# Row maxima of a block-sparse attention kernel taken from products of high parts, in two 64-row tiles of TensorE, from the twelfth unit on

## The chip, the cores and the metric

The program runs on one core of a Trainium2 chip. The time is the device time of one execution in microseconds (us); several executions are taken and their median is compared. A core has TensorE (PE in the profile; its weight loads are listed apart as PEld), VectorE (DVE), ScalarE (ACT), GpSimd (POOL) and SyncE (SP, which issues nearly all DMAs here). TensorE multiplies a stationary operand of up to 128 rows and 128 columns, the weights, with a moving operand that streams past it; results go to PSUM.

## The reference

Attention with a block mask, over 4 batches, 8 heads, 768 positions and a head size of 64, and then a two-layer network over the joined heads:

```
scores = scale * q @ k.T                       # 768 x 768 for each batch and head
mask   = neighbours, first and last block of 32, and 3 sampled blocks for each block of queries
scores = where(mask, scores, -1e9)
scores = scores - max(scores, axis=-1)
attn   = exp(scores) / (sum(exp(scores)) + 1e-9)
x      = attn @ v                              # heads joined: 3072 x 512
h      = x @ w_in                              # 3072 x 2048
out    = (h * clip(h + 3, 0, 6) / 6) @ w_out   # 3072 x 512
```

The row maximum cancels out of `attn` up to rounding: any number near it serves to keep `exp` in range.

## The kernel before, in words

**Number formats.** Most products are made in two or three parts. A value x is split into a high part (x rounded to fp32r, a format that TensorE takes in one pass) and a low part (x minus its high part, again fp32r). The products of attention weights with v (`av`) and the sums of exponentials (`dm`) take plain fp32 operands.

**Units.** The attention is done in 64 units, u0 to u63, one for each batch, half of the queries (384 of them) and head. A unit's steps are methods of the class `Unit`:

- `loadq`, `loadk`, `loadv`: DMAs on SP's queue. q arrives transposed and stacked twice, so that partitions 0 to 63 and 64 to 127 hold the same 64 x 384 numbers (`qraw`, one buffer, so that the next `loadq` waits for the last reader of this one). k likewise (`kraw`).
- `qh` (ACT) writes q/8 rounded, its high part, into all 128 partitions of `QA`; `ql` (DVE) then overwrites partitions 0 to 63 with the low part. `kh` (ACT) writes k's high part into both halves of `KA`. So one product of QA with KA over 128 rows gives (low q + high q) x high k.
- `m_0`, `m_1`, `m_2` (line 573): for a third of the unit's queries each, two matmuls with QA as weights and KA moving, 384 columns of keys each, into the two PSUM banks of one tile named `big`. Query 3p+t stands in row p of third t, so the weights are read with a step of three elements. Units 1 to 8 use other PSUM tiles (`early`).
- `r_0` to `r_2` (DVE) reduce each `big` tile to the maxima of the 24 blocks of keys; `fin` adds the mask and reduces to one maximum for each query, `mt` brings the maxima as a row into `qb` (by a DMA from the tenth unit on).
- `s_0` to `s_2`: the scores themselves, transposed, four matmuls each: KA x QA, and `kb` x `qb`, which holds low k x high q, the mask and the maxima in 97 rows. `e` (ACT) takes exp of each `big` tile of scores into `pr` (a pool of 14 buffers).
- `av` (line 636): 12 products of two units at once, one unit's result in PSUM partitions 0 to 63, the other's in 64 to 127, that is, in two column tiles of TensorE of 64 columns; `dm` (line 648): sums over keys for four rows at once, in four column tiles of 32. Both are fp32, so each product is two instructions.

**The network** runs as 64 steps, m0 to m63: `h_00` to `h_11` (x times w_in, 384 columns, three matmuls for each of four pieces), `ga`, `gb`, `gh`, `gl` (activation and split), `o_00` to `o_21` (times w_out, 512 columns, three matmuls each). The weights are split into parts in the first quarter of the run (steps w0 to w31).

**What sets the order.** The string `SCORE` lists every step of every unit in the order that a planner gave them; `play` (line 823) walks it and each engine issues in exactly that order. A step that has not been issued when something needs it is issued then. The pool `big` has two tiles, so `m`, `s`, `h` and `dm` share two PSUM tiles of two banks.

Of the kernel before, what the change touches and what calls it, by code (L numbers as in the profile page):

```python
# [35 lines left out]
BYDMA = 10  # L36
QUICK = "0 1 2 3 4 5 6 7 8 9 10 11 12 13 14 15 16 17 18 19 20 21 22 23 24 25 26 27 28 29 30 31"
# [8 lines left out]
    loadk kh kl qb; u1 fin_0; w2 bits_2; u2 ql m_0; w1 low; w0 high; w3 load; u0 e_2; u1 fin_1 mt qm; u2 r_0; w3
    size; u2 m_1; k0 kb_1; u1 s_0; u2 r_1; u1 s_1; w3 bits_0 bits_1 bits_2; u2 m_2 r_2; u1 e_0 e_1; w5 load size
    bits_0; u1 s_2 e_2 dm; u2 fin_0; w5 bits_1; u3 loadq qh ql qb loadk kh; u2 loadv fin_1 mt qm; w5 bits_2; w4 load;
    u0 loadv; u1 dc; u3 m_0 r_0; u2 s_0; w0 low; u3 m_1 r_1; u2 e_0; u4 loadq; w6 load; w4 size bits_0 bits_1; u2 s_1
    s_2 e_1 e_2; u3 m_2 r_2 fin_0; w4 bits_2; w3 high; w6 size; w3 low; u3 fin_1 kl; u4 loadk; w6 bits_0; w2 high; u1  # L50
    av; u4 qh ql; u1 rg rc; u3 mt; u4 qb; w6 bits_1; w1 save; u4 kh kl; u3 qm; u4 m_0; u3 s_0 e_0; u1 uc; w7 load; u4
    r_0 m_1 r_1; u3 s_1 s_2; w6 bits_2; u4 m_2; w7 size; u3 e_1 e_2; u4 r_2 fin_0; w7 bits_0; u3 av; u4 loadv; u5
    loadq qb qh; u4 fin_1 mt; u5 loadk kh; w7 bits_1 bits_2; w6 high; u5 ql m_0; w2 low; w8 load; u5 r_0; w3 save; u3
    uc; w8 size; w10 load; w8 bits_0 bits_1; w6 low; w8 bits_2; u4 qm; w7 high; u3 dm dc; u5 m_1 r_1; u4 s_0 s_1; w5
    high; u4 e_0; u1 rs; u5 m_2 r_2 kl; w10 size; u4 e_1; u6 loadq; u5 fin_0 fin_1; u4 s_2; u6 qh loadk ql kh; u5 mt
    qm; u6 m_0 r_0; u5 s_0; w7 low; u4 e_2; u6 m_1 r_1 kl qb; u5 e_0; w8 high; u5 s_1; w9 load; u3 rg; w5 low; u5
    s_2; w10 bits_0; u5 loadv; w6 save; u6 m_2; u5 e_1 e_2 dm; w9 size; u1 rb; u6 r_2 fin_0 fin_1 mt; w10 bits_1
    bits_2; u3 rc; u5 dc; u7 loadq qh; u5 av; u7 ql loadk kh m_0; w12 load; w9 bits_0 bits_1; u7 qb; u3 rs; w9
    bits_2; u6 qm; w4 high; u6 s_0 e_0; u7 kl; u8 loadq; u7 r_0; w4 low; u6 s_1; u7 m_1 r_1; u6 s_2; u7 m_2 r_2
    fin_0; u6 e_1; u8 qb; u6 e_2; u8 loadk; u5 rg; u7 loadv fin_1 mt; u8 qh; u6 loadv; u8 ql; u5 rc; u8 kh m_0 r_0;  # L60
    u7 qm; w8 low; w12 size; u5 uc; u7 s_0 e_0; w9 high; u8 m_1 r_1; w11 load size; u5 rs; u7 s_1; u1 ux_0; u7 s_2
    e_1 e_2; u9 loadq; w4 save; w11 bits_0; w12 bits_0; u8 m_2 r_2; w11 bits_1; w12 bits_1; u8 kl; u9 qh qb; u3 rb;
    u1 ux_1; u7 av; w11 bits_2; w12 bits_2; w5 save; u5 rb; u8 fin_0 fin_1 mt; w9 low; u9 ql; u7 dm; u5 ux_0; u1
    ux_2; w12 high low; u9 loadk; w14 load; u8 qm; u9 loadv kh; u7 dc; u9 kl m_0 r_0; w16 load; u9 m_1 r_1; w14 size
    bits_0; u8 s_0 s_1; w7 save; w2 save; w10 high; m0 loadin_0; w10 low; w14 bits_1; w11 high; w9 save; u10 loadq;
    w8 save; u8 e_0 s_2; u7 rg; u8 e_1 e_2; u10 qb; u9 m_2; u3 ux_0; w14 bits_2 high; u5 ux_1; w11 low; u7 rc; u9 r_2
    fin_0; w14 low; u9 fin_1; u10 loadk; u9 mt; u10 qh kh ql; u9 qm; m1 loadin_1; w16 size; m1 loadin_0; u5 ux_2; u10
    kl m_0 m_1 r_0 r_1; w12 save; u7 rs; w16 bits_0; u3 ux_1; u7 uc; u9 s_0 e_0 s_1 e_1; w16 bits_1; w18 load size;
    u3 ux_2; m0 h_00 loadin_1; w14 save; u11 loadq; w16 bits_2; w18 bits_0 bits_1; w11 save; u7 rb; w16 high; u9 s_2;
    m0 loadout_1; w10 save; u7 ux_0; m0 h_10; u9 e_2; u7 ux_1; m0 loadout_0; u10 m_2; w18 bits_2; u7 ux_2; u8 loadv;  # L70
    u10 r_2; u11 qh; w18 high low; u11 ql; m0 h_01; u10 fin_0; u11 qb; m0 h_11 ga; u11 loadk; w13 load; u11 loadv;
    w13 size; w15 load size; u11 kh; m1 h_00 h_10; w16 low; m1 loadout_1; u10 fin_1 mt loadv; w16 save; m0 gb gh; m1
    h_01 h_11; w13 bits_0 bits_1 bits_2; w15 bits_0; m0 gl; m3 loadin_1; w15 bits_1 bits_2; w13 high low; u10 qm s_0
    e_0; w17 load; w18 save; u9 av; m1 ga gb; w15 high low; w19 load; w17 size bits_0 bits_1; u9 dm dc; u12 loadq;
    u10 s_1; w19 size bits_0; m0 o_00; u10 e_1 s_2 e_2; w17 bits_2 high; m2 loadin_1; u11 m_0; m0 o_10 o_20; u11 kl;
    m1 gh gl; u12 loadv; m2 loadin_0; w13 save; w19 bits_1; u12 loadk; w20 load; w15 save; m2 loadout_0; u12 qh kh;
    u11 r_0; w19 bits_2; u12 qb; u11 m_1 r_1; m1 loadout_0; u11 m_2; m0 o_01 o_11; u9 rg; w22 load; w17 low; m2 h_00
    h_01; u12 kl ql; u11 r_2; w19 high; u13 loadk loadq; w20 size bits_0; u11 fin_0; w20 bits_1 bits_2; u11 fin_1;
    w17 save; m2 h_10 h_11; u12 m_0; u11 mt; m0 o_21; m1 o_00; w21 load; u13 loadv; m2 loadout_1; u12 r_0; m2 ga gb;
    w20 high; w22 size; m2 gh; m1 o_10; w22 bits_0; u12 m_1 r_1 m_2 r_2 fin_0; m4 loadin_1; u12 fin_1 mt qm; m1 o_20;  # L80
    w20 low; w22 bits_1; m1 o_01; m3 loadin_0; u11 qm s_0 s_1; w19 low; m1 o_11; u11 e_0 e_1; w21 size; w22 bits_2;
    w21 bits_0; m3 loadout_0; u11 s_2; m2 gl; u13 qh; u11 e_2; u13 ql; m1 o_21; w22 high; w21 bits_1 bits_2; u13 qb;
    w20 save; w24 load; m2 o_00; u13 kh kl; u14 loadq; w22 low; m2 o_10; u12 s_0 s_1; w22 save; u12 e_0 e_1; m2 o_01;
    u13 m_0 r_0; u12 s_2 suma; m2 o_11; u9 uc; u12 e_2; w24 size; u13 m_1; m3 h_00 h_10; u13 r_1; u14 qh; w24 bits_0
    bits_1 bits_2; u13 m_2; u14 ql; m3 h_01; u14 loadk kh kl; w26 load; u13 r_2; w19 save; w23 load; u13 fin_0; m3
    h_11; w21 high; u13 fin_1; m4 loadin_0; u13 mt; m3 ga gb; w0 save; w26 size bits_0; m5 loadin_0; u13 qm; w21 low
    save; w26 bits_1 bits_2; u14 m_0; u11 av; u14 r_0; u11 dm; u14 qb loadv; m5 loadin_1; w28 load; w23 size; w24
    high; w23 bits_0 bits_1; u12 sumb; u11 dc; m2 o_20; w26 high; u14 m_1 r_1; u12 sumc; m3 gh; w26 low; w24 low; u13
    s_0; w23 bits_2; u13 e_0; u15 loadq; m2 o_21; u13 s_1 e_1; m4 h_00 h_10; u15 loadk; u14 m_2; m4 h_01 h_11; w26
    save; u14 r_2; w30 load; u14 fin_0 fin_1 mt; u13 suma; u9 rc; w28 size bits_0; m3 loadout_1 gl; u11 uc; m4 ga gb;  # L90
    u13 s_2; u15 qb; u9 rs; m4 loadout_1; w23 high low save; u13 e_2 av; m4 gh; w28 bits_1; u15 qh; w28 bits_2; u15
    ql kh kl m_0; w30 size; u14 qm; u15 m_1 r_0 r_1; m3 o_00; u15 loadv; m3 o_10; u14 s_0 e_0; w30 bits_0; w27 load;
    u14 s_1 e_1; w27 size; m3 o_20; u13 sumb; m4 loadout_0; u13 uc; u16 loadq; m3 o_01; u11 rg; w24 save; u13 sumc;
    u15 m_2; u16 loadk; m5 h_00 h_10; u15 r_2; m4 gl; w30 bits_1; u9 rb; w30 bits_2; u14 s_2; w28 high; w27 bits_0;
    u15 fin_0 fin_1; u16 qb; m5 h_01; w31 load; u15 mt; u11 rc; u16 qh ql; w27 bits_1; u14 e_2; w28 low; u16 kh kl;
# [775 lines left out]
```

## Time and profile before

| | us |
|---|---|
| median of 3 runs | 958.35 |
| lowest and highest | 954.04, 960.99 |
| the profiled execution | 959.63, of which 957.8 from the first to the last instruction |
| PE busy | 927.6 |
| DVE busy | 601.9 |
| ACT busy | 442.4 |
| POOL busy | 243.3 |

Busy time of PE counts overlapping matmuls once. A matmul's recorded duration includes its way through the array, so a row of "338 ns" for 384 columns does not say how often one can start; the starts in the timeline do.

### The profile page before, as it was taken

The page shows a single profiled execution, that of the slowest core. Times are in us where ns is not written, and L with a number is a line of the kernel's source. Part 1 is how long each engine was busy: PE and PEld are TensorE (multiplying, and loading weights), DVE is VectorE, ACT ScalarE, POOL GpSimd, SP SyncE. Part 2 cuts the span into 40 slices and gives each one's busy share as a digit, 9 for nine tenths or more (in the row PEclk, how much of TensorE's full clock was granted, in tenths as well). Part 3 has the DMA queues.
Part 4 walks back from the last instruction along what each step waited for, and adds up shares of the span by engine and source line. Part 5 has one row for each costly group of instructions (what it writes and reads, how often), then busy time and mean ns, then how long its engine had stood idle before and what let it go on. Part 6 is the DMA issues. An engine that isn't in the chain of part 4 may idle for free.

```text
span 957.8 us, 13375 instructions
## 1 busy us (share of the span) xinstructions
PE 927.6 (97%) x4894; PEld 766.2 (80%) x4894; DVE 601.9 (63%) x875; ACT 442.4 (46%) x674; POOL 243.3 (25%) x145
## 2 busy tenths in 40 slices
...
GB/s 228 203 179 245 230 308 228 231 221 192 126 126 173 143 145 129 177 104 178 149 143 125 172 175 103 147 140 163 184 103 155 164 150 140 125 147 72 187 110 88
DMA packets 97125, 155.84 MB, mean 163 GB/s; under 512 B 24618, under 2 KB 45226, under 8 KB 97060
## 3 DMA queue, kind: packets, MB, share of 16 engines
...
q8 instruction: 38, 0.62, 0.3%
...
## 4 chain that ended last, share of the span: by engine, by line
PE 86%; DVE 6%; DMA 4%; issue 1%; ACT 1%; POOL 0%; SPq 0%; ACTq 0%; DVEq 0%
PE big L321 48%; PE out L321 28%; PE av L321 10%; DVE bm L321 2%; DVE xhl L321 2%; DVE QA L321 1%; DMA kraw<-kT 1%; DMA wout_lo<-xhl 1%; DMA wraw<-w_out 1%; DVE acc L321 0%; DMA qb<-mneg 0%; DMA vo<-vP 0%; ACT KA L321 0%; DMA spread<-rec 0%; DVE spread L321 0%
## 5 line engine op out<-in xcount | busy, mean ns | idle before, releaser
L321 PE MATMUL big<-xhl,win_hi 128*128 128x384 f32 x1024 | 263.2, 338 | 0.0
L321 DVE TENSOR_REDUCE bm<-big 128x24 f32<-128x768 f32 x168 | 159.6, 954 | 139.1 <-PE big L321 137.3
L321 POOL TENSOR_TENSOR glo<-g,ghi 128x768 fp32r<-128x768 f32 x64 | 120.4, 1882 | 398.3 <-ACT ghi L321 382.1
L321 ACT ACTIVATE pr<-big 128x768 f32<-128x768 f32 x192 | 151.7, 811 | 129.1 <-PE big L321 128.5
L321 POOL TENSOR_TENSOR kb<-kraw,KA 64x768 fp32r<-64x768 f32 x64 | 121.4, 1897 | 306.5 <-ACT KA L321 263.3
L321 PEld LDWEIGHTS big<-xhl,win_hi 128*128 128x128 f32 x1024 | 187.5, 188 | 4.9 <-issue 1.2
L321 PE MATMUL big<-xhl,wlo_in 128*128 128x384 f32 x512 | 173.6, 339 | 0.0
L321 PE MATMUL out<-wout_hi,ghi 128*128 128x512 f32 x384 | 151.7, 395 | 0.0
L321 PE MATMUL out<-wout_hi,glo 128*128 128x512 f32 x384 | 151.4, 394 | 0.0
L321 PE MATMUL out<-wlo_out,ghi 128*128 128x512 f32 x384 | 151.2, 394 | 0.0
L321 PE MATMUL big<-QA,KA 128*128 128x384 f32 x384 | 136.3, 355 | 0.7 <-DVE bm L321 0.5
L321 PE MATMUL big<-qb,kb 97*128 97x384 f32 x384 | 134.8, 351 | 0.7 <-DMA qb<-mneg 0.4
L321 ACT ACTIVATE g<-big,half_b 128x768 f32<-128x768 f32 x64 | 57.7, 902 | 161.3 <-PE big L321 140.5
L321 PE MATMUL av<-pr,vo 128*64 128x384 f32 x768 | 131.4, 492 | 0.0
L321 DVE SCALAR_TENSOR_TENSOR g<-g,big 128x768 f32<-128x768 f32 x64 | 60.7, 949 | 97.7 <-ACT g L321 97.7
L321 PEld LDWEIGHTS av<-pr,vo 128*64 128x64 f32 x768 | 52.5, 137 | 65.8 <-issue 64.3
L321 PE MATMUL big<-KA,QA 128*128 128x384 f32 x336 | 91.0, 358 | 10.1 <-ACT KA L321 5.3
L321 PEld LDWEIGHTS big<-KA,QA 128*128 128x128 f32 x336 | 75.8, 255 | 27.3 <-issue 8.0
L321 PEld LDWEIGHTS big<-xhl,wlo_in 128*128 128x128 f32 x512 | 96.4, 188 | 0.0
L321 PEld LDWEIGHTS out<-wout_hi,glo 128*128 128x128 f32 x384 | 72.1, 188 | 16.7
L321 PEld LDWEIGHTS big<-QA,KA 128*128 128x128 f32 x384 | 75.9, 198 | 10.5 <-issue 2.5
L321 ACT CAST ghi<-g 128x768 fp32r<-128x768 f32 x64 | 53.3, 833 | 63.7 <-PE out L321 32.0
...
## 6 DMA issues: line engine op xcount, KB each, us to landing
...
```

The lines of the kernel that those rows point to most:

```text
L321: return lambda *a, **k: tc.keep_in_program_order(op(*a, **k))
```

## The change

Units below 12 are as before. From unit 12 on, a new step `qt` (ACT) writes the high part of q once more, into a tile `QT` of all 128 partitions, sorted so that the queries of one third stand side by side. `m_t` then makes its two matmuls from QT and KA over 64 rows each: the first from partitions 0 to 63 for the keys 0 to 383, the second from partitions 64 to 127 for the keys 384 to 767. The low part of q is left out of these maxima. So `m_0` needs `qt` and `kh` but no longer `ql`, which `s_0` needs now. `pr` has 13 buffers in place of 14. `SCORE` is a new order of all steps.

```
+HALVES = 12
...
-    k0 maskload samp; u0 loadq loadk qh; k0 idload; w0 load; k0 table; u0 qb kh kl ql m_0 m_1; k0 index; u0 r_0; w0
+    k0 samp; u0 loadq; k0 table; u0 qh ql; k0 index maskload; u0 loadk kh m_0 m_1 r_0 qb; w0 load; k0 idload allow_0;
...
-            "m_0": "ql kh", "m_1": "m_0", "m_2": "m_1", "r_0": "m_0", "r_1": "m_1 r_0", "r_2": "m_2 r_1",
+            "qt": "loadq", "m_0": "kh", "m_1": "m_0", "m_2": "m_1", "r_0": "m_0", "r_1": "m_1 r_0", "r_2": "m_2 r_1",
...
-            "s_0": "qm qb kl", "s_1": "s_0", "s_2": "s_1", "e_0": "s_0", "e_1": "s_1 e_0", "e_2": "s_2 e_1",
+            "s_0": "qm ql qb kl", "s_1": "s_0", "s_2": "s_1", "e_0": "s_0", "e_1": "s_1 e_0", "e_2": "s_2 e_1",
...
+            self.halves = n >= HALVES
...
+            if op == "m_0":
+                out.append((self, "qt" if self.halves else "ql"))
+            if op == "qt":
+                out.append((prev2, "m_2"))
...
+        def qt(self):
+            self.QT = sb.tile([P, HALF], F32R, name="QT")
+            act.mul(out=self.QT.rearrange("d (t p) -> d t p", t=NT), in_=self.qraw.rearrange("d (p t) -> d t p", t=NT), mul=0.125)
...
-                pe.matmul(out_j, lhsT=self.QA[:, t:HALF:NT], rhs=self.KA[:, j * HALF:(j + 1) * HALF], start=True, stop=True)
+                k = self.KA[:, j * HALF:(j + 1) * HALF]
+                if self.halves:
+                    q, k = self.QT[64 * j:64 * j + 64, t * P:(t + 1) * P], k[64 * j:64 * j + 64]
+                else:
+                    q = self.QA[:, t:HALF:NT]
+                pe.matmul(out_j, lhsT=q, rhs=k, start=True, stop=True)
...
-            self.pr[cp] = sb.tile([P, 2, HALF], F32, name="pr", bufs=14)
+            self.pr[cp] = sb.tile([P, 2, HALF], F32, name="pr", bufs=13)
```

Where the instructions stand: first TensorE somewhat before the middle, where unit 31 has its maxima. Before (`big<-KA,QA` is one step `m`, both of its matmuls; `out` and `wout`, `wlo` are the network's second layer, `xhl` its first):

```order
L321 MATMUL big_3894<-KA_3875,QA_3844 128x384 x2
L321 MATMUL out0_3508<-wout_hi_73,ghi_3734 128x512
L321 MATMUL out0_3508<-wlo_out_3826,ghi_3734 128x512
L321 MATMUL out0_3508<-wout_hi_73,glo_3735 128x512
L321 MATMUL out1_3509<-wout_hi_73,ghi_3734 128x512
L321 MATMUL out1_3509<-wlo_out_3826,ghi_3734 128x512
L321 MATMUL out1_3509<-wout_hi_73,glo_3735 128x512
L321 MATMUL big_3906<-KA_3875,QA_3844 128x384 x2
L321 MATMUL big_3912<-xhl_3103,win_hi_72 128x384 x2
```

and the same unit in the changed kernel, where `KA,QT` are the products in half-row tiles:

```order
L320 MATMUL out1_3548<-wout_hi_73,glo_3760 128x512
L320 MATMUL big_3943<-KA_3855,QT_3887 128x384 x2
L320 MATMUL big_3946<-KA_3855,QT_3887 128x384 x2
L320 MATMUL out2_3549<-wout_hi_73,ghi_3759 128x512
L320 MATMUL out2_3549<-wlo_out_3692,ghi_3759 128x512
L320 MATMUL out2_3549<-wout_hi_73,glo_3760 128x512
L320 MATMUL out0_3547<-wout_hi_73,ghi_3759 128x512
L320 MATMUL out0_3547<-wlo_out_3715,ghi_3759 128x512
L320 MATMUL out0_3547<-wout_hi_73,glo_3760 128x512
L320 MATMUL big_3962<-xhl_3268,win_hi_72 128x384 x2
```

Two of the unit's three steps `m` have moved together, with six matmuls of 128 rows behind them; the third stands alone later. Over the whole order 156 steps `m` are in half-row tiles, in 124 places: 92 steps by themselves and 32 times two in a row. Before, 6 of these 156 steps stood directly behind another step `m`. Counted over TensorE's order, weights of 128 columns follow on matmuls of another tile shape (64-row tiles, or column tiles) 253 times, and 38 times before.

On ACT at the same unit, before (`QA<-qraw` is `qh`, `qb<-qraw` the copy for the second score product, `KA<-kraw` is `kh`, `pr` the exponentials, `ghi` and `g` the network's activation):

```order
L321 ACTIVATE qb11_109<-qraw_3741 64x384
L321 ACTIVATE QA_3844<-qraw_3741 128x384
L321 COPY uu_3848<-av_3743 128x384
L321 ACTIVATE pr_3850<-big_3815 128x768
L321 ACTIVATE g_3852<-big_3802,half_b_114 128x768
L321 CAST KA_3875<-kraw_3800 128x768
```

and in the changed kernel, with `QT<-qraw` as `qt`:

```order
L320 CAST KA_3855<-kraw_3808 128x768
L320 CAST ghi_3759<-g_3758 128x768
L320 ACTIVATE pr_3870<-big_3865 128x768
L320 ACTIVATE QT_3887<-qraw_3844 128x384
L320 ACTIVATE QA_3889<-qraw_3844 128x384
L320 ACTIVATE pr_3903<-big_3892 128x768
L320 ACTIVATE qb11_109<-qraw_3844 64x384
L320 ACTIVATE g_3913<-big_3872,half_b_114 128x768
```

`qt` is one more pass over q on ACT, put ahead of `qh`; there are 52 of them.

## Rows read from the trace of the kernel before

**Rows 1.** The page: busy time of the engines over the span (share of the span, instructions).

```profile
PE 927.6 (97%) x4894; PEld 766.2 (80%) x4894; DVE 601.9 (63%) x875; ACT 442.4 (46%) x674; POOL 243.3 (25%) x145
```

**Rows 2.** Busy time of the engines in stretches of the span (start:end, length; busy us and instructions of PE, PEld, DVE, ACT, POOL; then granted clock of TensorE, share of the DMA engines, GB/s).

```profile
0.00:50.00 50.00, 37.69 (x191) 25.87 (x195) 40.41 (x82) 35.30 (x58) 14.08 (x23) 0.97 0.67 214
50.00:100.00 50.00, 40.66 (x219) 26.14 (x208) 42.48 (x80) 34.53 (x57) 9.11 (x5) 0.84 0.75 215
...
200.00:400.00 200.00, 198.22 (x1051) 169.20 (x1047) 125.12 (x172) 90.72 (x136) 54.50 (x29) 1.00 0.47 149
400.00:600.00 200.00, 200.00 (x1066) 165.94 (x1066) 126.98 (x170) 87.78 (x134) 53.35 (x29) 1.00 0.48 149
```

**Rows 3.** The chain of work that ended last: its share of the span by engine.

```profile
PE 86%; DVE 6%; DMA 4%; issue 1%; ACT 1%; POOL 0%; SPq 0%; ACTq 0%; DVEq 0%
```

**Rows 4.** Timeline of TensorE, matmuls of the network and one step `m` (start us, us, engine, line, operation, out<-in, rows*columns of the weights, rows x columns of the moving operand, count). A row of x2 holds two that overlap.

```profile
501.15 0.40 PE L321 MATMUL out<-wlo_out,ghi 128*128 128x512 f32 x1
501.39 0.40 PE L321 MATMUL out<-wout_hi,glo 128*128 128x512 f32 x1
501.62 0.52 PE L321 MATMUL big<-KA,QA 128*128 128x384 f32 x2
501.98 0.51 PE L321 MATMUL big<-xhl,win_hi 128*128 128x384 f32 x2
```

**Rows 5.** Timeline of TensorE, one step `s`, with the row of the network behind it.

```profile
520.31 0.34 PE L321 MATMUL big<-QA,KA 128*128 128x384 f32 x1
520.49 0.34 PE L321 MATMUL big<-qb,kb 97*128 97x384 f32 x1
520.66 0.34 PE L321 MATMUL big<-QA,KA 128*128 128x384 f32 x1
520.85 0.34 PE L321 MATMUL big<-qb,kb 97*128 97x384 f32 x1
521.02 0.39 PE L321 MATMUL out<-wout_hi,ghi 128*128 128x512 f32 x1
```

**Rows 6.** Timeline of TensorE's matmuls and weight loads behind a `dm` in four column tiles, and around an `av` in two.

```profile
425.37 0.85 PE L321 MATMUL big<-acc,ones 128*32 128x384 f32 x8
426.16 0.44 PE L321 MATMUL big<-QA,KA 128*128 128x384 f32 x1
426.44 0.34 PE L321 MATMUL big<-qb,kb 97*128 97x384 f32 x1
...
510.59 0.33 PE L321 MATMUL big<-xhl,wlo_in 128*128 128x384 f32 x1
510.85 0.20 PEld L321 LDWEIGHTS av<-pr,vo 128*64 128x64 f32 x4 [0.25 <-issue]
510.85 4.09 PE L321 MATMUL av<-pr,vo 128*64 128x384 f32 x24
511.23 0.14 PEld L321 LDWEIGHTS av<-pr,vo 128*64 128x64 f32 x2 [0.18 <-issue]
...
514.13 0.14 PEld L321 LDWEIGHTS av<-pr,vo 128*64 128x64 f32 x2 [0.18 <-issue]
...
514.87 0.69 PE L321 MATMUL big<-KA,QA 128*128 128x384 f32 x2
...
515.22 0.19 PEld L321 LDWEIGHTS out<-wout_hi,ghi 128*128 128x128 f32 x1
```

**Rows 7.** Timeline of TensorE around products whose weights have two columns (`ident,mneg`, fp32r operands like those of `KA,QA`): matmuls and then weight loads where 128-column weights stand behind them, and weight loads where they follow on a `dm` of fp32 operands.

```profile
37.74 0.34 PE L321 MATMUL big<-ident,mneg 128*2 128x128 f32 x3
37.92 0.62 PE L321 MATMUL out<-KA,QA 128*128 128x384 f32 x2
...
37.74 0.15 PEld L321 LDWEIGHTS big<-ident,mneg 128*2 128x2 f32 x3 [0.60 <-ACT KA L321]
37.86 0.43 PEld L321 LDWEIGHTS out<-KA,QA 128*128 128x128 f32 x2
...
62.19 0.13 PEld L321 LDWEIGHTS big<-pr,ones 128*32 128x32 f32 x4 [0.19 <-issue]
62.95 0.14 PEld L321 LDWEIGHTS big<-ident,mneg 128*2 128x2 f32 x3 [0.62 <-issue]
```

**Rows 8.** Groups of weight loads by form (busy us, mean ns | idle before).

```profile
L321 PEld LDWEIGHTS big<-xhl,win_hi 128*128 128x128 f32 x1024 | 187.5, 188 | 4.9 <-issue 1.2
...
L321 PEld LDWEIGHTS big<-KA,QA 128*128 128x128 f32 x336 | 75.8, 255 | 27.3 <-issue 8.0 <-ACT KA L321 6.6 <-ACT g L321 2.7
```

**Rows 9.** Groups of TensorE's matmuls by form from 150 to 900 us (busy us, mean ns | idle before, and what ended it).

```profile
L321 PE MATMUL big<-KA,QA 128*128 128x384 f32 x300 | 79.3, 349 | 3.8 <-DVE QA L321 1.7 <-DVE bm L321 1.2 <-DVE mneg L321 0.8
```

**Rows 10.** Groups by form over the whole span: ACT's pass over q, an ACT copy with a step in its output, DVE's pass for the low part, and the reduction of one `big` tile.

```profile
L321 DVE TENSOR_REDUCE bm<-big 128x24 f32<-128x768 f32 x168 | 159.6, 954 | 139.1 <-PE big L321 137.3
...
L321 DVE SCALAR_TENSOR_TENSOR QA<-qraw,QA 64x384 fp32r<-64x384 f32 x64 | 46.5, 727 | 26.0 <-ACT QA L321 25.8
...
L321 ACT ACTIVATE QA<-qraw 128x384 fp32r<-128x384 f32 x64 | 33.2, 519 | 11.0 <-PE big L321 10.5 <-DMA qraw<-qT 0.5
...
L321 ACT CAST qb<-big 1x384 fp32r<-1x384 f32 x10 | 6.7, 666 | 5.7 <-PE big L321 5.6
```

**Rows 11.** Waits of SP's queue: who waited for whom, us in total, times, longest us (`DVE QA` is `ql`, waited for by the next unit's `loadq`).

```profile
SPq L321 <- DVE mneg L321: 119.0, 40, 11.2
SPq L321 <- DVE QA L321: 72.7, 26, 8.5
```

More of the change, by code (lines that the diff above doesn't have):

```diff
@@ L46 @@
[L46 to L95, printed above, removed]
@@ L101 @@
-    av; m5 loadout_0; m8 loadin_1; m7 loadin_0; u11 rb; w25 high; w27 save; m7 loadin_1; m6 ga; u16 e_0; w29 load;
-    u18 loadq; u15 suma sumb; m6 gb gh gl; u15 sumc dm dc; w25 low; m5 o_00; u16 s_1; w31 bits_1; u16 s_2 e_1 suma;
-    u18 loadk; u16 e_2 sumb; m5 o_10; u11 ux_0 ux_1; m6 loadout_1; w25 save; u15 rg; m7 h_00; u11 ux_2; u15 rc; m7
-    h_01; m6 loadout_0; u17 m_0 r_0; u15 rs; u13 rb; w29 size; u9 ux_1; m7 h_10 h_11; w29 bits_0; u9 ux_2; w29
-    bits_1; w31 bits_2 high; u15 rb; w29 bits_2 high low; w31 low; m5 o_20; m9 loadin_0; m5 o_01 o_11 o_21; w31 save;
@@ new lines @@
+    mq; u0 r_2; k0 rows; u0 kl; u1 qb qh ql loadk; w0 high; u1 kh; k0 qb_00; u2 loadv; k0 qb_01 qb_11 qb_10 ident mqc
+    kb_0; u1 loadv; k0 kb_1; w1 bits_0; u1 m_0; w2 load; u1 kl; u0 fin_0 fin_1 mt; u1 r_0; u0 qm; w1 bits_1; u1 m_1
+    r_1; w2 size; u2 loadq; u0 s_0 e_0; w1 bits_2; u1 m_2 r_2; w2 bits_0 bits_1; u1 fin_0; w1 high; u0 s_1 s_2 e_1;
+    u2 qh loadk kh; w3 load; w2 bits_2; u2 ql m_0; w1 low; u0 e_2; u1 fin_1; u0 loadv; u2 qb; u1 mt; w5 load; u2 r_0;
+    u1 qm; u2 m_1 r_1; w3 size bits_0 bits_1 bits_2; u1 s_0 e_0 s_1; u3 loadq; u2 m_2; u1 e_1 s_2; w5 size; u1 e_2
@@ new lines @@
+    dm; u3 qb qh; u2 r_2 fin_0 kl; w5 bits_0 bits_1; u3 loadk kh; u2 fin_1 mt qm; u3 loadv; w4 load; u3 ql m_0; w5
+    bits_2; u2 s_0; u3 r_0; u4 loadq; u1 dc; u3 m_1; u2 e_0; w4 size; u2 s_1 s_2; w2 high; w5 high; u3 r_1 m_2; w0
+    low; u1 av; u2 e_1 e_2; w4 bits_0; u3 kl; u4 qh; w4 bits_1; w6 load size; u4 loadk kh kl; u1 rg; u3 r_2 fin_0
+    fin_1 mt; w4 bits_2; w6 bits_0; u4 ql m_0; w6 bits_1; u3 qm; w7 load; u4 qb r_0; u3 s_0 e_0; w6 bits_2; u4 m_1
+    r_1; u3 s_1 s_2; u1 rc; w3 high low; u4 m_2 r_2; u1 uc; u3 e_1; w7 size bits_0; u3 e_2 av; u5 loadq qh; u4 fin_0;
@@ new lines @@
+    w7 bits_1 bits_2; u5 loadk qb kh ql; u4 fin_1; w2 low; w8 load; u4 mt; w6 high; w8 size; u5 m_0 r_0; u4 qm; u3 uc
+    dm; w8 bits_0; u5 m_1; u3 dc; u4 s_0 s_1 e_0; w10 load size; u4 e_1; w8 bits_1; w6 low; w8 bits_2; u5 r_1 m_2 kl
+    r_2 fin_0; u1 rs; u5 fin_1; u4 s_2; u6 loadq qh loadk; u5 mt; u6 kh; u4 loadv; u5 qm; u4 e_2; u6 qb ql m_0; u5
+    s_0 e_0; u6 r_0; w10 bits_0; u6 m_1 r_1; u5 s_1; w10 bits_1; u5 loadv; u6 loadv; w6 save; u5 s_2; w10 bits_2; u6
+    m_2 r_2 fin_0 fin_1; w12 load; u3 rg; w7 high; u6 kl; u5 e_1 e_2; u7 loadq; w8 high; w12 size; w7 low; w12
@@ new lines @@
+    bits_0; u5 dm dc; u6 mt; u3 rc; w9 load; u6 qm; u1 rb; u6 s_0; u7 loadk; w12 bits_1; u7 qb qh ql; u3 rs; w12
+    bits_2; u6 e_0; w9 size; u6 s_1; w9 bits_0 bits_1; u6 s_2; u5 av; u7 kh kl loadv m_0; u6 e_1; w9 bits_2 high; w4
+    high; u6 e_2; u1 ux_0; w9 low; w12 high; u8 loadq; w0 save; u5 rg; u8 qb; u7 r_0; u8 loadk; w7 save; u8 qh; u7
+    m_1 r_1 m_2; u1 ux_1; u7 r_2; u1 ux_2; u7 fin_0 fin_1; w9 save; u7 mt; w14 load; u5 uc; u8 kh ql m_0; w5 low; u7
+    qm; u8 r_0; u7 s_0 e_0; u8 m_1 r_1; u7 s_1; w8 low; u3 rb ux_0; u9 loadq; u5 rc; u7 s_2 e_1; w11 load; u8 m_2
@@ new lines @@
+    r_2; u9 qh; u7 e_2 av; u8 kl; u9 qb; w14 size; u8 fin_0; w11 size; u5 rs; u9 loadk; w4 low; w5 save; w4 save; w11
+    bits_0; u8 fin_1 mt qm; u9 kh; w8 save; w11 bits_1; m1 loadin_1; u9 ql; w14 bits_0; w11 bits_2; w14 bits_1; u8
+    loadv; u7 dm dc; u5 rb; u9 m_0 kl r_0; u10 loadq; w10 high; w12 low; u3 ux_1; w10 low; u3 ux_2; w14 bits_2; w11
+    high; w16 load; u7 rg; u5 ux_0; w11 low; u8 s_0 e_0 s_1; u10 loadk; u8 s_2 e_1 e_2; u9 m_1 r_1; u7 rc; w16 size;
+    w18 load; u10 qb qh ql; u9 m_2 r_2; u10 kh; w12 save; u9 fin_0 fin_1 mt qm; w16 bits_0; u7 uc rs; w10 save; u11
@@ new lines @@
+    save; m2 h_01 h_11; m4 loadin_0; w22 load; u11 r_2 fin_0; m0 o_11; u12 qt; w20 bits_1; m2 loadout_0; u11 fin_1;
+    m0 o_21; u12 qb m_0; m1 o_00 o_10; u12 ql; w20 bits_2; m2 ga gb; u12 r_0; u13 loadk; m4 loadin_1; m2 gh; w22
+    size; u12 m_1 r_1; w17 save; u11 mt; u13 loadq; u12 m_2; w21 load; m2 gl; u12 r_2 fin_0; u13 qt; m1 o_20 o_01;
+    u11 qm s_0 s_1 e_0 loadv; m3 loadin_0; m1 o_11; u13 loadv; u11 s_2 e_1; w21 size; u12 fin_1; u13 qh; u12 mt; w19
+    low; w22 bits_0 bits_1 bits_2; m1 o_21; u12 loadv; u13 qb; m2 o_00; u11 e_2; w19 save; u12 qm; u13 ql; u12 s_0
@@ new lines @@
+    m2 o_20; w26 high; u13 s_0 e_0 s_1; w21 low; w23 bits_0; u13 e_1; u15 loadk; w26 low; u15 loadq; w20 save; u12
+    sumb; m3 loadout_0; w28 load; m2 o_21; w23 bits_1; m3 gh; m4 h_00; u14 m_2 r_2; u11 uc rg; m4 loadout_1 h_10; w26
+    save; w3 save; m4 h_01; u14 fin_0; w23 bits_2; u15 qt; w28 size; u14 fin_1; w23 high; u9 rc; w28 bits_0; u12
+    sumc; m3 gl; w28 bits_1 bits_2; u13 s_2 e_2; u15 qh; m4 h_11 ga gb gh gl; w23 low; u11 rc; u15 ql; u13 av; u15 kh
+    kl m_0 m_1; m3 o_00; u15 r_0 r_1; m3 o_10; u13 uc; u15 qb; w27 load; m5 loadin_0; u14 mt qm s_0; m3 loadout_1;
```

402 lines of the change are left out of this document (210 added, 192 removed).

## The prediction

> **What bounds the kernel now.** I looked first at the page's busy shares: PE is busy for 97% of the span, DVE for 63%, ACT for 46% [rows 1]. A share is an average, so I read it by stage next. In the first 100 us PE is busy for 37.7 and 40.7 us of 50 while DVE has 40 to 42 us: that start is not PE's. From 200 us on PE has 198.2 and 200.0 us of 200, at a granted clock of 1.00, with DVE and ACT at two thirds and less [rows 2]. The chain of waits says the same: 86% of it is PE [rows 3]. Since a busy row also counts a matmul's way through the array, I looked at starts. In a step `s` they are 0.18, 0.17, 0.19 and 0.17 us apart, 0.71 us for four matmuls of 384 columns: a slot of 0.1775 us [rows 5]. The step `m` beside the network takes two such slots: 501.62 to 501.98 [rows 4]. And between 150 and 900 us PE idled only 3.8 us ahead of all 300 matmuls of `m` [rows 9]. So from unit 12 on PE issues one matmul behind another, and the time there is the sum of slots. What takes a slot away shortens the kernel; a slot that comes empty lengthens it.
>
> **The change, part by part.**
>
> Slots. 156 steps `m` (52 units of three) are touched. If the two 64-row tiles run side by side, a step takes one slot in place of two: 156 x 0.1775 = 27.7 us less. The trace shows no row tiles. The nearest rows are the column tiles of `av`: weight loads come two at a time, and from 511.23 to 514.13 there are nine rounds of two matmuls, 0.32 us each. In `dm` eight matmuls, two rounds of four tiles, take from 425.37 to 426.16, 0.79 us: two rounds of 0.32 and 0.15 for the edges. A round costs the same with four tiles as with two, so tiles do run at once here [rows 6]. I take the full 27.7; the other end is 0.
>
> Weight reads. The weights of `KA,QA` are read with a step of three, and load in 255 ns against 188 for weights side by side [rows 8]. QT is sorted, so its loads should take the 188. This matters only where a load is not hidden, directly behind column tiles; some 18 steps `m` stand so before: 18 x 0.067 = 1.2 us, I take 1 us less. Against that, a half-row step needs two loads ahead of it in one slot. If they don't overlap, some of the second shows: a load behind column tiles puts 0.28 us (426.16 to 426.44) where a slot is 0.1775, so about 0.105 us is a load's own length, two are 0.21, and 0.03 us stick out, at 124 places 4 us. In `av` the loads go in pairs, so the low end is 0; I take 2 us.
>
> Changing the tile shape. This is the term that decides. Entering `av`, the next matmul starts 0.26 us after the last (510.59 to 510.85), not 0.1775, and its weights are not loaded ahead (0.25 us idle on PEld). Leaving it, the last round starts at 514.13 + 0.32 = 514.45 and the next matmul at 514.87: 0.42 us and not 0.32. The first 128-column load behind column tiles is bare: 0.28 us to the next start and not 0.18 (426.16 to 426.44). So one change into 128-column weights costs 0.10 + 0.10, more closely 0.195 us [rows 6]. The order has 253 such changes, 38 before: 215 more, at most 215 x 0.195 = 41.9 us. The low end is 0, and rows speak for it: the `ident,mneg` products have two-column weights, a smaller tile too, but three of them and the `KA,QA` behind them start within 0.18 us (37.74 to 37.92), 0.06 us each, and its load begins at 37.86, while they still stream: nothing was emptied. Where the same products follow on a `dm`, they do pay: from the loads of its last round at 62.19 to theirs at 62.95 it is 0.76 us for two rounds of 0.32 [rows 7]. What differs is the operands: `av` and `dm` are fp32 and take two passes, `ident` and `KA,QA` are fp32r. The price hangs on the fp32 groups at least as well as on the tile's shape, and the new tiles are fp32r, like their neighbours, with their rows where the 128-row products have theirs. I take 0 and keep 41.9 for the range.
>
> The Trainium skill, TensorEngine Tiling (Array Packing), section Key Properties, says otherwise: changing the tiling mode drains TensorE. By that, the sum would be 41.9 us higher; the trace agrees at every edge of `av` and `dm` (0.26 and 0.42 us) and does not show it at `ident` (0.06 us).
>
> ACT's `qt`. 52 passes at 519 ns are 27 us; with a step in the access the nearest row is 666 ns, so up to 35 us [rows 10]. ACT goes from 46% to 49% or 50%. It costs nothing as long as PE has other work queued: it is ahead of `m_0` but `ql` (727 ns on DVE behind `qh`) leaves that chain, so the way from q's landing to `m_0` becomes shorter by about 0.7 us. What stands behind `qt` in ACT's queue at unit 31 are `qh`, an exponential and `g`; each is late by 0.5 us, and PE waits for `g`'s successors or a free `big` only if the order left them no slack. The row of 3.8 us idle says it leaves enough [rows 9]. Without that cover the price is 52 x 0.52 = 27 us; I take 0.
>
> DVE reduces a `big` tile in 0.954 us [rows 10]; of two steps `m` in a row the second tile is free after 1.9 us. At unit 31 six matmuls of 512 columns, 1.4 us, and then a step `h` stand behind, which needs a `big` tile: 0.5 us could show at such places, 32 x 0.5 = 16 us at most. The free tile comes after 1.0 us already and `h` needs one only; 0. The next unit's `loadq` waits for the last reader of `qraw`, and behind it on SP's queue wait the loads of the network's weights; SP waited 72.7 us for `ql` already without PE idling for a DMA, and `qt` comes ahead of `qh` and `ql`, so it is not the last reader: 0 [rows 9, 11]. One `pr` buffer less: 0, since the exponentials wait for PE, not for room. The new order at the start: PE idles 21.7 us of the first 100 [rows 2]; a new order may move that by some 4 us to either side; 0.
>
> Sum, against the profiled execution: 959.6 - 27.7 - 1 + 2 = 932.9 us. The median of the runs is 1.3 us below the profiled one, so 932 us.
>
> **Rivals.** (1) Slower: the change of tile shape costs what it costs at `av`. Then 932 + 41.9 = 974 us. It decides as soon as one change costs over 27.7 / 215 = 0.13 us, two thirds of the row. For it: each edge of `av` and `dm` shows it. Against it: `ident`, and that no fp32 is involved.
> (2) Half of the price: the array is emptied but the next load is ahead, or only one of the two directions pays. 215 x 0.10 = 21 us: 953 us. For it: the two halves of the price are separate in the rows (0.10 empty, 0.10 load).
> (3) The change doesn't do what it says: the two tiles run one after another, without a price for changing. Then the 27.7 us don't come: 932 + 27.7 = 960 us. Against it: four tiles of `dm` take no longer than two of `av`.
> (4) Both (1) and (3): over 1000 us.
>
> **How the numbers follow.** Forecast, tiles at once and no price worth a slot: 0.48, 932 us, by itself 926 to 941 (the 4 us of loads and of the start to either side). Rival 1: 0.27, 965 to 980. Rival 2: 0.13, 941 to 963. Rival 3: 0.07. Rival 4: 0.05. A range of 926 to 976 leaves out rival 4, the upper third of rival 1 and 0.03 below, 0.17 in all. A measurement of this kernel can tell about 1% from no change, 948.8 to 967.9 us. Faster: the forecast and a third of rival 2, 0.52. Within 1%: two thirds of rival 2, rival 3 and the low edge of rival 1, 0.19. Slower: 0.29.
>
> **What the profile will show.** Step by step: in the timeline the two `KA,QT` matmuls of a step start within a few hundredths of a us of each other (else rival 3); the next start behind them is 0.18 us later and loads of the neighbours are ahead on PEld (the forecast), or 0.26 us later with idle time on PEld and a bare load (rival 1). The loads of `KA,QT` should be near 188 ns, not 255. ACT has 52 instructions more and near 27 us more. PE's busy time from 200 us on stays at its full share, at the same clock; if instead PE idles ahead of `m` for want of `qt`, or of `h` for want of a `big` tile, one of my zeros was wrong. The forecast falls if PE's matmuls around `KA,QT` are further apart than two slots.

## The result, and the profile after

The changed kernel took 967.88 us (median of 4 runs, 966.75 to 968.25) against 956.54 us for the kernel before beside it: a ratio of 1.0111 (95% interval 1.0086 to 1.0136). It is 11.3 us slower where 27 us less were forecast. The forecast of 932 us, by itself 926 to 941, did not come. The time lies inside the range of 926 to 976 us only because that took in most of rival 1 (965 to 980 us), where it fell.

| us | before, profiled | after, profiled |
|---|---|---|
| the execution | 959.63 | 968.25 |
| first to last instruction | 957.8 | 966.5 |
| PE busy | 927.6 | 937.9 |
| DVE busy | 601.9 | 585.1 |
| ACT busy | 442.4 | 472.2 |

The page of the changed kernel, with the busy time of its engines and then the shares of the chain that ended last (against [rows 1, 3]):

```profile
PE 937.9 (97%) x4894; PEld 724.6 (75%) x4894; DVE 585.1 (61%) x875; ACT 472.2 (49%) x726; POOL 247.5 (26%) x145
...
PE 91%; DMA 3%; ACT 2%; DVE 2%; issue 1%; POOL 1%; DVEq 0%; SPq 0%; ACTq 0%
```

Nothing took the place of PE. ACT has its 52 passes and 30 us more, DVE has less, and the chain is more PE's than before. Next its windows, columns as in [rows 2]:

```profile
0.00:50.00 50.00, 38.55 (x205) 26.12 (x206) 39.37 (x86) 35.67 (x59) 15.08 (x23) 0.97 0.67 208
50.00:100.00 50.00, 38.91 (x201) 24.91 (x201) 40.90 (x79) 33.82 (x56) 9.11 (x5) 0.87 0.68 214
...
200.00:400.00 200.00, 200.00 (x1042) 156.73 (x1041) 125.91 (x171) 97.98 (x149) 56.22 (x29) 1.00 0.48 150
400.00:600.00 200.00, 200.00 (x1050) 152.73 (x1048) 118.32 (x168) 95.75 (x147) 51.42 (x27) 1.00 0.47 145
```

Read the counts, not the busy times. PE is busy for all of 200 us in both middle stages, at a granted clock of 1.00 as before, and yet it gets through 1042 and 1050 matmuls where it did 1051 and 1066 [rows 2]. If the change had brought a slot for each step, the counts would have gone up. (Two orders do not have quite the same instructions in a window; full_rows below has the order of the changed kernel.) PE waits for nobody; its matmuls are further apart. The start of the run is no cause: PE idles 22.5 us of the first 100, and 21.7 before.

The timeline shows where they are further apart. First one half-row step by itself, in the middle of the network's first layer, matmuls and then weight loads:

```profile
326.21 0.34 PE L320 MATMUL big<-xhl,wlo_in 128*128 128x384 f32 x1
326.48 0.44 PE L320 MATMUL big<-KA,QT 64*128 64x384 f32 x2
326.85 0.62 PE L320 MATMUL big<-xhl,win_hi 128*128 128x384 f32 x2
327.31 0.34 PE L320 MATMUL big<-xhl,wlo_in 128*128 128x384 f32 x1
...
326.48 0.19 PEld L320 LDWEIGHTS big<-KA,QT 64*128 64x128 f32 x2 [0.25 <-issue]
326.85 0.30 PEld L320 LDWEIGHTS big<-xhl,win_hi 128*128 128x128 f32 x2 [0.19 <-issue]
327.13 0.19 PEld L320 LDWEIGHTS big<-xhl,wlo_in 128*128 128x128 f32 x1
```

The two matmuls stand in one row of x2, since they overlap: by the single records of the trace (one for each instruction; a row merges several) their starts are 4 ns apart, and 2 to 5 ns at the other places shown. So the tiles do run at once. But the step starts 0.27 us behind the last matmul and not 0.18; the next matmul starts 0.37 us behind the step; and of the two matmuls there (x2, 0.46 us to the next row) the first takes 0.28. On PEld both loads, into the half-row tiles and out of them, stand with idle time ahead of them (0.25 and 0.19 us, "issue": they waited for nothing that the profile shows) and begin with their matmul instead of ahead of it. That is what [rows 6] show at the edges of `av`: 0.25 us of idle PEld and a bare load. The two loads of a pair take 0.19 us together, no longer than one.

Two half-row steps in a row, among the matmuls of 512 columns:

```profile
322.97 0.39 PE L320 MATMUL out<-wout_hi,glo 128*128 128x512 f32 x1
323.29 0.62 PE L320 MATMUL big<-KA,QT 64*128 64x384 f32 x4
323.84 0.50 PE L320 MATMUL out<-wout_hi,ghi 128*128 128x512 f32 x1
324.17 0.39 PE L320 MATMUL out<-wlo_out,ghi 128*128 128x512 f32 x1
324.40 0.39 PE L320 MATMUL out<-wout_hi,glo 128*128 128x512 f32 x1
```

They pay the same once for both: 0.32 us to enter (the slot here is 0.23), 0.55 us for two pairs and the emptying behind them, 0.33 us for the first matmul behind them. The groups by form that answer to [rows 8, 9, 10]:

```profile
L320 PE MATMUL big<-KA,QT 64*128 64x384 f32 x312 | 60.9, 419 | 0.7 <-DVE bm L320 0.7
...
L320 PEld LDWEIGHTS big<-KA,QT 64*128 64x128 f32 x312 | 26.9, 183 | 45.3 <-issue 30.8 <-ACT pr L320 2.0 <-ACT KA L320 1.8
...
L320 ACT ACTIVATE QT<-qraw 128x384 fp32r<-128x384 f32 x52 | 37.6, 722 | 7.6 <-DMA qraw<-qT 7.6
...
L320 DVE TENSOR_REDUCE bm<-big 128x24 f32<-128x768 f32 x168 | 157.6, 953 | 111.7 <-PE big L320 111.0
```

PE idled 0.7 us in all ahead of the 312 half-row matmuls, and what ended that was DVE, so `qt` is never late, although it takes 722 ns.

### The profile page after: what moved, and what is told of

It is laid out like the page before. It is cut to its first block, busy times and chain, and to the rows that moved or that the text cites. A ratio compares the mean times of both kernels' runs of the same rounds, so it can differ in the third digit from the quotient of the medians.

```text
span 966.5 us, 13439 instructions
## 1 busy us (share of the span) xinstructions
PE 937.9 (97%) x4894; PEld 724.6 (75%) x4894; DVE 585.1 (61%) x875; ACT 472.2 (49%) x726; POOL 247.5 (26%) x145
## 4 chain that ended last, share of the span: by engine, by line
PE 91%; DMA 3%; ACT 2%; DVE 2%; issue 1%; POOL 1%; DVEq 0%; SPq 0%; ACTq 0%
PE big L320 49%; PE out L320 29%; PE av L320 13%; DMA qraw<-qT 1%; DMA kraw<-kT 1%; DVE bm L320 1%; DMA wraw<-w_in 1%; DMA krows_d<-krows 1%; DVE QA L320 1%; POOL kb L320 1%; ACT pr L320 0%; ACT qb L320 0%; ACT KA L320 0%; ACT xhl L320 0%; ACT QA L320 0%
## 5 line engine op out<-in xcount | busy, mean ns | idle before, releaser
L320 PE MATMUL big<-xhl,win_hi 128*128 128x384 f32 x1024 | 266.4, 341 | 0.0
L320 DVE TENSOR_REDUCE bm<-big 128x24 f32<-128x768 f32 x168 | 157.6, 953 | 111.7 <-PE big L320 111.0
L320 POOL TENSOR_TENSOR kb<-kraw,KA 64x768 fp32r<-64x768 f32 x64 | 125.1, 1955 | 322.4 <-ACT KA L320 292.0
L320 PEld LDWEIGHTS big<-xhl,win_hi 128*128 128x128 f32 x1024 | 185.3, 188 | 11.1 <-issue 6.6
L320 PE MATMUL out<-wout_hi,ghi 128*128 128x512 f32 x384 | 159.3, 415 | 0.0
L320 DVE TENSOR_TENSOR acc<-pr 128x768 f32<-128x768 f32 x52 | 56.5, 1087 | 59.0 <-ACT pr L320 58.5
L320 PEld LDWEIGHTS out<-wout_hi,ghi 128*128 128x128 f32 x384 | 72.0, 188 | 26.7 <-issue 18.3
L320 PEld LDWEIGHTS big<-QA,KA 128*128 128x128 f32 x384 | 75.3, 196 | 12.6 <-issue 2.4
```

The costliest lines, as they stand in the source:

```text
L320: return lambda *a, **k: tc.keep_in_program_order(op(*a, **k))
```

## The experiments

Three explanations stood against each other. **A:** each change of tile shape costs about 0.2 us, as at `av` (rival 1). **B:** the new order, `qt` or the missing `pr` buffer costs the time, and the tiles nothing. **C:** each half-row step costs something by itself, so the price goes by steps and not by changes. Every time stands beside that of the kernel before on the same chip.

| run | half-row steps | us | ratio to before |
|---|---|---|---|
| changed kernel | 156 | 967.88 | 1.0111 [1.0086, 1.0136] |
| full_rows | none | 956.14 | 0.9992 [0.9978, 1.0005] |
| doubles_only | 64, two in a row | 955.21 | 0.9982 [0.9967, 0.9997] |
| singles_only | 92, alone | 969.66 | 1.0124 [1.0101, 1.0147] |
| few | 23, where a change is due anyway | 954.75 | 0.9978 [0.9965, 0.9991] |
| old_order | 156, in the order of before | 980.48 | 1.0248 [1.0222, 1.0275] |
| old_order_full | none, in the order of before | 958.57 | 1.0018 [1.0002, 1.0034] |

**full_rows: all but the tiles.** The changed kernel, but the steps `m` read QT over all 128 rows, two slots each. QT then counts the high part twice, so it is scaled by 1/16.

```
-  mul=0.125)                                                    # in qt
+  mul=0.0625)
...
-  q, k = self.QT[64 * j:64 * j + 64, t * P:(t + 1) * P], k[64 * j:64 * j + 64]
+  q = self.QT[:, t * P:(t + 1) * P]
```

> The changed kernel with its order, its qt and its 13 pr buffers, but each step m from unit 12 on reads the sorted QT over all 128 rows in one 128x128 tile (q scaled by 1/16, so that the two equal halves add up to the same maxima). Theory A, the price of changing the tile's shape: 215 changes of about 0.2 us and 156 slots of 0.1765 us go and come back, worked out over the whole order as 15.0 us less than the changed kernel, so 953 us, some 3 us under the kernel before. Theory B, the new order, qt on ACT or the pr buffer cost the time: it stays at 965 to 968 us.

956.14 us (954.65 to 958.37): 11.7 us less than the changed kernel (11.4 by the two ratios), and the same as before. Theory A had forecast 15.0. The order, `qt` and the buffer together cost nothing that can be told, and B falls. `qt` takes as long here as in the changed kernel. With the same order, PE gets through 20 and 14 matmuls more in the two middle stages than the changed kernel does:

```profile
200.00:400.00 200.00, 200.00 (x1062) 169.61 (x1061) 131.10 (x177) 99.47 (x151) 56.27 (x29) 1.00 0.48 151
400.00:600.00 200.00, 199.84 (x1064) 163.61 (x1063) 121.42 (x169) 96.50 (x147) 53.08 (x28) 1.00 0.47 146
```

The timeline of this kernel gives the comparison that the trace of before could not, the same two places with full rows:

```profile
323.27 0.34 PE L320 MATMUL big<-xhl,wlo_in 128*128 128x384 f32 x1
323.44 0.51 PE L320 MATMUL big<-KA,QT 128*128 128x384 f32 x2
323.79 0.52 PE L320 MATMUL big<-xhl,win_hi 128*128 128x384 f32 x2
324.14 0.34 PE L320 MATMUL big<-xhl,wlo_in 128*128 128x384 f32 x1
...
320.08 0.39 PE L320 MATMUL out<-wout_hi,glo 128*128 128x512 f32 x1
320.31 0.85 PE L320 MATMUL big<-KA,QT 128*128 128x384 f32 x4
321.00 0.39 PE L320 MATMUL out<-wout_hi,ghi 128*128 128x512 f32 x1
321.23 0.39 PE L320 MATMUL out<-wlo_out,ghi 128*128 128x512 f32 x1
```

The step by itself: 323.27 to 324.14 is 0.87 us with full rows; 326.21 to 327.31 is 1.10 us with half rows, though a slot less is used. It loses 0.22 to 0.23 us. Two in a row: 320.08 to 321.23 is 1.15 us, and 322.97 to 324.17 is 1.20 us. They lose 0.05 us with two slots saved.

**doubles_only and singles_only: the same tiles with many changes and with few.** A set of names (unit and third) says which steps are in half-row tiles; the others read full rows. The maxima of the latter are doubled, which cancels.

```
-  if self.halves:
+  if self.halves and f"{self.n}.{t}" in TILED:      # the 64 steps that stand two in a row, or the other 92
...
+  elif self.halves:
+      q = self.QT[:, t * P:(t + 1) * P]
```

> As the changed kernel, but only the 64 steps m that stand two in a row are in half-row tiles; the 92 that stand alone read QT over all 128 rows (their maxima come out doubled, which cancels in the softmax). Theory A (a price for each change of shape, whatever stands between): 15.6 us less than the changed kernel, 952 us, level with full_rows. Theory C (a price for each half-row step, not for the change): 64 of 156 steps keep the loss, 959 us. Theory B: 965 to 968 us.

> The other way round: the 92 steps m that stand alone are in half-row tiles, the 64 that stand two in a row read QT over all 128 rows (maxima doubled there). Theory A: 0.6 us more than the changed kernel, 968 us, though 64 steps fewer are tiled. Theory C: 92 of 156 steps keep the loss, 962 us. Theory B: 965 to 968 us.

955.21 us (953.45 to 956.76) and 969.66 us (967.41 to 970.25). Against full_rows the 64 steps two in a row bring 0.9 us, hardly more than the scatter, and the 92 single steps cost 13.5 us. A price per step would have divided the 11.7 us as 64 to 92, so C falls. The two parts add up to 12.6 us, close to the 11.7 of both together. It is the number of changes that counts.

**old_order and old_order_full: the order of before.** Half-row tiles in the order of steps that the kernel before has, `qt` put in directly behind `qh`, 13 `pr` buffers; and the same with full rows of QT. There only 6 of the 156 steps stand behind another, so nearly every step pays for itself.

```
-  SCORE = """ ... """         # the changed kernel's
+  SCORE = """ ... """         # that of the kernel before, "qt" behind "qh" for each unit from 12 on
```

> The half-row tiles of the changed kernel in the order of the kernel before (qt put directly behind qh, 13 pr buffers). There 150 of the steps m stand by themselves or behind something else, 6 of 156 behind another m. Theory A, a price of about 0.2 us for each change of shape: 26.8 us over the kernel before, worked out over that order, so 984 us: the new order is what keeps the changed kernel's loss at a third of that. If the new order was itself a cost, this one would be faster than the changed kernel, under 968 us.

> The order of the kernel before, with qt and 13 pr buffers, each step m from unit 12 on over all 128 rows of the sorted QT (q scaled by 1/16): neither tiles nor the new order. Theory A: 1.0 us under the kernel before, 956 us, which cannot be told from it. If qt on ACT or the missing pr buffer cost something, it is above the kernel before by that.

980.48 us (978.53 to 983.3) and 958.57 us (955.29 to 961.76). The tiles cost 21.9 us in this order, the new order halves that to 11.7 by putting steps `m` in pairs, and without the tiles both orders are within 0.3% of each other, by their ratios to the kernel before. So the new order is the part of the change that limits the loss. Theory A's sizes came out too large here too: it had put old_order 26.8 us over the kernel before, and 24.0 were measured; doubles_only it had put 15.6 us under the changed kernel, and 12.7 were. And old_order_full was to be level with the kernel before or 1 us below it; its ratio of 1.0018 is some 1.7 us more, with an interval just above 1, so a small cost of `qt` or of the missing buffer in the order of before is not excluded.

**edges and edges2: what is it that pays?** Both are full_rows with a few units in other forms, looked at for the starts in the timeline alone. In edges, units 20 and 21 make both matmuls from rows 0 to 63 (no second tile beside them), 24 and 25 both from rows 64 to 127, 28 and 29 take all rows as plain fp32, and in 32 and 33 each full product is followed by a second one with 64 of its columns as weights. In edges2 the second product has 64 columns in fp32 (units 20, 21), or 32 rows (units 28, 29; these maxima lack half of the terms).

```
+  if form == "low rows":    q, k = q[:64], k[:64]
+  elif form == "high rows": q, k = q[64:], k[64:]
+  elif form == "fp32":      q, k = q.bitcast(F32), k.bitcast(F32)
   pe.matmul(out_j, lhsT=q, rhs=k, start=True, stop=True)
+  if form == "64 columns":
+      pe.matmul(out_j[:64], lhsT=q[:, :64], rhs=k, start=True, stop=True)
+  if form == "fp32, 64 columns":                                           # edges2
+      pe.matmul(out_j[:64], lhsT=q[:, :64].bitcast(F32), rhs=k.bitcast(F32), start=True, stop=True)
+  elif form == "32 rows":                                                  # edges2
+      pe.matmul(out_j, lhsT=q[:32], rhs=k[:32], start=True, stop=True)
```

> As full_rows, but a few units have their maxima in other forms, to read the edges in the timeline: units 20, 21 both matmuls from rows 0 to 63, units 24, 25 both from rows 64 to 127, units 28, 29 over all rows with fp32 operands (two passes), units 32, 33 over all rows with a second matmul of 64 weight columns behind each. If every change of the tile's shape empties the array, the start behind the last 128-row matmul of 384 columns is 0.26 us later and the next load is bare at units 20, 21, 24, 25 and around the 64-column ones. If only tiles that lie beside each other do, the starts there stay at 0.18 us. If a change of the number format alone does it, units 28, 29 show 0.26 us on entering and about 0.42 on leaving, with the tile unchanged; if not, 0.18 and 0.32.

> As full_rows, with a second matmul behind each of the maxima of a few units: units 20, 21 with 64 weight columns in fp32, the form of av but at its first place alone; units 28, 29 with rows 0 to 31 alone (their maxima are then those of a part of the product, which cancels). In the run named edges 64 fp32r columns and a change of format alone both came at the plain slot, and 64 rows alone paid. If the price of av is that of a narrow fp32 tile, the start before and behind the 64 fp32 columns is 0.09 us late and the next load bare; if it is that of two tiles side by side, the starts are plain (0.18 before, about 0.32 behind). 32 rows should pay as 64 rows did: 0.26 us to the next start and 0.28 behind a bare load.

968.78 and 980.5 us, one execution each. Timeline of edges: rows 0 to 63 alone, rows 64 to 127 alone (with an `av` behind them), all rows in fp32, and 64 fp32r columns behind full products, with the loads of the last. A row that holds several matmuls shows the shape of the first.

```profile
248.95 0.39 PE L321 MATMUL out<-wout_hi,glo 128*128 128x512 f32 x1
249.27 0.61 PE L321 MATMUL big<-KA,QT 64*128 64x384 f32 x2
249.81 0.50 PE L321 MATMUL out<-wout_hi,ghi 128*128 128x512 f32 x1
250.15 0.40 PE L321 MATMUL out<-wlo_out,ghi 128*128 128x512 f32 x1
...
306.27 0.33 PE L321 MATMUL big<-xhl,wlo_in 128*128 128x384 f32 x1
306.54 0.62 PE L321 MATMUL big<-KA,QT 64*128 64x384 f32 x2
307.08 0.54 PE L321 MATMUL av<-pr,vo 128*64 128x384 f32 x2
...
355.60 0.40 PE L321 MATMUL out<-wout_hi,glo 128*128 128x512 f32 x1
355.83 1.45 PE L321 MATMUL big<-KA,QT 128*128 128x384 f32 x4
356.83 0.69 PE L321 MATMUL out<-wout_hi,ghi 128*128 128x512 f32 x1
357.36 0.39 PE L321 MATMUL out<-wlo_out,ghi 128*128 128x512 f32 x1
...
413.21 0.40 PE L321 MATMUL out<-wout_hi,glo 128*128 128x512 f32 x1
413.44 0.87 PE L321 MATMUL big<-KA,QT 128*128 128x384 f32 x4
414.15 0.51 PE L321 MATMUL big<-xhl,win_hi 128*128 128x384 f32 x2
...
413.21 0.72 PEld L321 LDWEIGHTS big<-KA,QT 128*128 128x128 f32 x4
```

A half-row tile with nothing beside it pays exactly what the pair of tiles pays: 0.32 us to enter, 0.54 for two matmuls (one behind the other here) and the emptying, 0.34 for the first one behind. Rows 64 to 127 enter at the same price, 0.27 us (306.27 to 306.54) where a slot of 384 columns is 0.18. So the price is not that of two tiles at once. All rows in fp32 pay nothing: the entry is the plain slot of 0.23 us, and from 355.83 to 357.36 it is 1.53 us, which is four passes of 0.32 us, the round of [rows 6], and one slot of 0.23 (the record of the matmul behind begins during the last pass, at 356.83). So the format alone is free. And 64 columns in fp32r pay nothing either: two full products and two with half of the columns take 0.71 us (413.44 to 414.15), four slots of 0.1775, and their loads run on from 413.21 while the matmul ahead still streams. So narrow fp32r weights cost no more than their slot.

Timeline of edges2: 64 fp32 columns, then 32 rows, each between full products.

```profile
254.50 0.40 PE L321 MATMUL out<-wout_hi,glo 128*128 128x512 f32 x1
254.74 2.29 PE L321 MATMUL big<-KA,QT 128*128 128x384 f32 x6
256.96 0.50 PE L321 MATMUL out<-wout_hi,ghi 128*128 128x512 f32 x1
...
367.06 0.40 PE L321 MATMUL out<-wout_hi,glo 128*128 128x512 f32 x1
367.29 1.44 PE L321 MATMUL big<-KA,QT 128*128 128x384 f32 x4
368.66 0.50 PE L321 MATMUL out<-wout_hi,ghi 128*128 128x512 f32 x1
369.00 0.39 PE L321 MATMUL out<-wlo_out,ghi 128*128 128x512 f32 x1
```

The same 64 columns in fp32 do pay: from 254.74 to 256.96 it is 2.22 us for two full slots and four passes, 0.36 + 1.29 = 1.64 us without a price; 0.58 us are left for the changes inside. 32 rows pay as 64 do: 1.37 us (367.29 to 368.66) for four matmuls worth 0.71 us. So two things were seen to pay here: fewer rows (64 or 32, tried in fp32r alone) and 64 columns in fp32. They pay the same 0.09 us of emptying; the bare load is 0.10 us for 128 columns and 0.05 for 64, as the first round of `av` shows (0.38 us from 510.85 to 511.23 where a round is 0.32 [rows 6]). The 97 rows of `qb,kb` between products of 128 rows pay nothing [rows 5].

**few: tiles only where the price is due anyway.** From A follows where the tiles are worth it: between two groups of column tiles, or beside one, where entering or leaving is paid for already. 23 of the 156 steps stand so in the new order, two in a row next to such a group or one between two.

```
-  if self.halves:
+  if self.halves and f"{self.n}.{t}" in TILED:      # 23 steps beside av and dm
```

> The changed kernel's order, with half-row tiles only at the 23 steps m where a change of shape is due anyway (they stand two in a row next to column tiles, or between two groups of them); all others read QT over all 128 rows (doubled maxima, which cancel). Theory A, worked out over the order: 1.8 us under full_rows and 1.2 us under doubles_only, so 954 us, 0.3% under the kernel before. If tiles never pay, it is level with full_rows at 956 us.

954.75 us (951.27 to 956.34), a ratio of 0.9978 (0.9965 to 0.9991). That is the lowest of all, 0.2% below the kernel before and, by the two ratios, 1.3% below the changed one; doubles_only is next. From full_rows and doubles_only it can't be told by its time, since the intervals overlap. The timeline shows the two sides of a group of `av`:

```profile
238.01 0.40 PE L323 MATMUL out<-wout_hi,glo 128*128 128x512 f32 x1
238.34 0.62 PE L323 MATMUL big<-KA,QT 64*128 64x384 f32 x4
238.88 4.09 PE L323 MATMUL av<-pr,vo 128*64 128x384 f32 x24
242.91 0.61 PE L323 MATMUL big<-KA,QT 64*128 64x384 f32 x4
243.45 0.49 PE L323 MATMUL out<-wout_hi,ghi 128*128 128x512 f32 x1
```

Each pair of steps stands against `av` on one side. The two pairs add two changes, some 0.4 us, and save four slots, 0.71 us. Over 23 steps that is about 2 us, no more. The traces of few and full_rows have the same order of matmuls; place by place, the 23 steps are 1.7 us shorter in few.

## Why the prediction was wrong

**The bound.** Right: PE stayed the bound at a granted clock of 1.00, and the count of starts decided, not the busy row.

**Slots, 27.7 us less.** Right. The pairs start 2 to 5 ns apart and a half-row step uses one slot, so rival 3 (960 us) and with it rival 4 fall.

**Changing the tile shape, taken as 0.** This is the step that failed. The price is that of the rows of `av`: by the starts, 0.095 us for the emptying and 0.105 us for the bare load at each change into 128-column weights. Rival 1 stood for it with 215 x 0.195 = 41.9 us. Less the slots, 14 to 15 us are left; measured were 11.3 us against before and 11.7 against full_rows. The Trainium skill's rule (TensorEngine Tiling (Array Packing), section Key Properties: changing the mode drains TensorE) agrees with all of these runs for row tiles (the next start 0.09 us late) and for narrow weights in fp32. Narrow weights in fp32r came at the plain slot, so either they are no change of mode or the rule does not hold for them; no run tells which.

How the wrong end came to be chosen: I had two rows that paid and one that didn't, and two differences between them, shape and number format. I gave the price to the format. The row that didn't pay, `ident` [rows 7], was narrow in columns and fp32r, and edges shows that fewer columns in fp32r cost nothing (64 columns: 0.71 us for four slots). So it said nothing about tiles with fewer rows. That the format alone is free was shown by the same run, and no row of before had it: an fp32 product with 128 columns between fp32r ones. With a confound that no row resolves, 0.48 against 0.27 was too much for the free end, all the more as the new tiles have fewer rows and `ident` has all of them.

**Rival 2, half of the price.** Falls: both halves are there at each change, the empty stretch and the bare load.

**Second load, +2 us.** Not needed: the two loads of a pair overlap (0.19 us for x2). **Straight weights, -1 us.** The loads became as short as said, 183 ns [rows 8]; their part of the sum is too small to be seen.

**`qt` at no cost.** Right about the time, wrong about the size: 722 ns lie above both rows that bounded it, 519 and 666 [rows 10], and ACT has 30 us more. PE's idle time ahead of `m` is 0.7 us. **Start, buffer, SP's queue, `big`, each 0.** Right as a sum in the new order: full_rows differs from before by less than can be told (0.9992).

**What stays open.** Counted over the whole order with these prices the tiles should cost 15.0 us against full_rows, and 11.7 were measured. The traces of the two kernels hold the same 4894 matmuls in the same order, so their starts can be compared one by one. From the matmul ahead of the tiles to the second one behind them, 67 single steps between full products lose 0.21 us on average, 20 pairs between full products 0.02 (the median is 0.05), and a single step beside a group of column tiles loses 0.02; a pair beside such a group gains 0.14 to 0.15. All 124 places together lose 13.0 us, so 15.0 was 2 us too much. Away from them the changed kernel is 1.7 us shorter, 0.6 of it ahead of the first tile; why is open. Nor was it tried whether fp32r products in two column tiles would pay, so why narrow fp32r weights cost nothing more is open.
